# A spectral filter and a gated unit in one kernel: shorter table arithmetic, filter loads without a cast on ScalarE's queue, and an emitted order kept on four engines

## The chip, the cores and the metric

The kernel runs on one core of a Trainium2 chip. The core has five engines that run their own instruction streams in order: PE (TensorE, matrix products), DVE (VectorE), ACT (ScalarE), POOL (GpSimd) and SP (SyncE, which here only issues transfers). Sixteen DMA engines move data for all of them. The metric is the device time of one execution in microseconds, and the number to forecast is the median over several runs.

## The reference, cut to what matters

```python
X = np.fft.rfft(x, axis=1)                    # x: 8 batches, 3200 positions, 256 channels, float32
Y = X * (filt_r + 1j * filt_i)[None]          # 1601 frequencies x 256 channels
y = np.fft.irfft(Y, n=3200, axis=1)           # first layer's output
gate = sigmoid(causal_conv(y, conv_w))        # 5 taps along the positions, per channel
out = ((gate * (y @ w_val)) @ w_out)          # 256 x 256 weights, float32 out
```

## The kernel before

**The transform.** 3200 is 128 x 25, so the transform of a batch is done in two passes of matrix products with tables of cosines and sines that the kernel builds itself. The first pass (`s1`) multiplies the input with the 128-point table `cf_t`; its result goes through a scratch tensor in DRAM, `dscr`, to be read back in another layout. The second pass (`s2`) uses `wc_t`, `ws_t` and `wsn_t`. The product with the filter (`fr_t`, and `fm_t`, which holds the imaginary part with both signs) is three instructions on VectorE: `za` (line 354), `zb` (358), `z` (360). The way back is `inva` with `vc_t`, `vs_t`, `vsn_t`, a second scratch tensor `escr`, and `invb` with `ci_t`. Then come `conv` (20 matmuls into one sigmoid), `val` and `outp`.

**The names.** Each batch is cut into seven chunks, so (b, j) below is chunk j of batch b. A chunk's transfers are called X (input load, line 86, issued by POOL, which casts float32 to bf16 on the way), D (write of `so` to `dscr`, line 312), T (read of `dscr` into `tt`, lines 326 to 329, eight transfers a batch), E (write of `u` to `escr`, line 392, two or three transfers a chunk), V (read of `escr` into `vt`, line 398, seven a batch) and O (output, line 475). SP issues all but X, so these five share one in-order queue.

**The loop.** One pass G of the loop emits, for chunks that are some passes apart, `load_x`, `invb`, `s2`, `conv`, `s1`, `inva`, `val`, `outp`. `s2` runs 9 passes behind `s1`, `inva` 10 and `invb` 19. All seven chunks of `dscr` are read back after the last `s1` of a batch, so T(b) has three passes to arrive before `s2`(b, 0); V(b) has three passes between the last `inva` and `invb`(b, 0).

**Buffers.** PSUM is a pool of four tiles of 128 x 1024 float32, one for each stage of a chunk in turn, so a stage can start when the tile of four stages before is evicted: `invb` needs the eviction of the `s1` before it (`so`, line 310, VectorE). ScalarE evicts `xs` (349), `u` (381), `y` (415) and the gate (436).

**What sets the order.** A scheduler orders the instructions of every engine by its own estimate of times, and then gives each transfer a completion counter. There are eight counters for the transfers of SP and ACT together, taken in turn, and eight for POOL's. A transfer waits until the previous holder of its counter has landed. SP, ACT and POOL stand still in such a wait.

**The preparation.** Before the loop the tables are made. VectorE reduces each angle by `floormod` (seven instructions, lines 103 to 113), ScalarE takes the sine, and VectorE spreads it (`expand`, line 171, 13 instructions a table) and negates it (177). POOL issues the seven X of batch 0, then the 24 filter loads (lines 216 to 225, with a cast to bf16), eight loads of weights (276, 280), and only then X of batch 1. The seven `so` of batch 0 stand on VectorE behind the tables of the second pass. The filter's signs are applied on VectorE (232, 234), as are the 20 `dg_t` instructions (284).

Of the kernel before, what the change touches and what calls it, by code (L numbers as in the profile page):

```python
# [8 lines left out]
FP32 = mybir.dt.float32  # L9
# [6 lines left out]
PI = math.pi  # L16
# [6 lines left out]
R = 25  # L23
# [12 lines left out]
def kernel(  # L36
# [31 lines left out]
    b_npi = cpool.tile([128, 1], FP32, name="b_npi")  # L68
# [5 lines left out]
    tpool = ctx.enter_context(tc.tile_pool(name="s2i", bufs=8))  # L74

# [13 lines left out]
    for j in range(NCH):  # L89
        load_x(0, j)  # L90


    with tc.tile_pool(name="gen", bufs=1) as g1, \
# [3 lines left out]
        def floormod(src_ap, divisor):  # L97
            shp = list(src_ap.shape)
            divi = g2.tile(shp, I32, name=f"fm_i{shp[1]}")
            bak = g2.tile(shp, FP32, name=f"fm_b{shp[1]}")  # L100
            q = g2.tile(shp, FP32, name=f"fm_q{shp[1]}")
            cm = g2.tile(shp, FP32, name=f"fm_c{shp[1]}")
            nc.vector.tensor_scalar(divi[...], src_ap, 1.0 / float(divisor), None,
                                    op0=ALU.mult)
            nc.vector.tensor_copy(bak[...], divi[...])
            nc.vector.scalar_tensor_tensor(q[...], bak[...], -float(divisor), src_ap,
                                           op0=ALU.mult, op1=ALU.add)
            nc.vector.tensor_scalar(cm[...], q[...], float(divisor) - 0.5, None,
                                    op0=ALU.is_ge)
            nc.vector.scalar_tensor_tensor(q[...], cm[...], -float(divisor), q[...],  # L110
                                           op0=ALU.mult, op1=ALU.add)
            nc.vector.tensor_scalar(cm[...], q[...], -0.5, None, op0=ALU.is_lt)
            nc.vector.scalar_tensor_tensor(q[...], cm[...], float(divisor), q[...],
                                           op0=ALU.mult, op1=ALU.add)
            return q

        def iota(shape, pattern, base, cm, name):
            t = g1.tile(shape, FP32, name=name)
            nc.gpsimd.iota(t[...], pattern=pattern, base=base, channel_multiplier=cm,
                           allow_small_or_imprecise_dtypes=True)  # L120
            return t

        nc.vector.memset(b_npi[:, :], -PI)
        pcol = iota([128, 1], [[0, 1]], 0, 1, "pcol")


        kc = iota([128, NG, 2, GL], [[5, NG], [0, 2], [1, GL]], 1, 0, "kc")
        nc.vector.memset(kc[:, NG - 1, 0, GL - 1:GL], 0.0)
        pr = g1.tile([128, NG, 2, GL], FP32, name="pr")
        nc.vector.tensor_scalar(pr[...], kc[...], pcol[:, 0:1], None, op0=ALU.mult)  # L130
        nc.vector.tensor_scalar(pr[:, :, 0, :], pr[:, :, 0, :], 0.75 * L, None,
                                op0=ALU.add)
        q = floormod(pr[...].rearrange("p g c l -> p (g c l)"), L)
        nc.scalar.activation(cf_t[:, :], q[...], AF.Sin, bias=b_npi[:, 0:1],
                             scale=2.0 * PI / L)
# [10 lines left out]
        rq = floormod(pcol[...], R)  # L146
        lp = g1.tile([128, 1], FP32, name="lp")
        nc.vector.tensor_tensor(lp[...], pcol[...], rq[...], op=ALU.subtract)
        nc.vector.tensor_scalar(lp[...], lp[...], 1.0 / R, None, op0=ALU.mult)
        rp = g1.tile([128, 1], FP32, name="rp")  # L150
        nc.vector.tensor_copy(rp[...], rq[...])
# [16 lines left out]
        def expand(dst, src):  # L168
            nc.gpsimd.memset(dst[:, :, P2:128], 0.0)
            for g in range(NG):  # L170
                nc.vector.tensor_tensor(
                    dst[:, g, 0:P2].rearrange("p (l r) -> p l r", l=GL),
                    src[:, g, :].unsqueeze(1).to_broadcast((128, GL, R)),
                    mk[...], op=ALU.mult)

        def negate(dst, src):
            nc.vector.tensor_scalar(dst[...], src[...], -1.0, None, op0=ALU.mult)

        def sincos(prod, dc, ds, dsn):
            qs = floormod(prod[...].rearrange("p g r -> p (g r)"), N)  # L180
            sn = g2.tile([128, NG, R], FP16, name="sn")
            nc.scalar.activation(sn[...].rearrange("p g r -> p (g r)"), qs[...],
                                 AF.Sin, bias=b_npi[:, 0:1], scale=2.0 * PI / N)
            pc = g2.tile([128, NG, R], FP32, name="pc")
            nc.vector.tensor_scalar(pc[...], prod[...], 0.75 * N, None, op0=ALU.add)
            qc = floormod(pc[...].rearrange("p g r -> p (g r)"), N)
            cs = g2.tile([128, NG, R], FP16, name="cs")
            nc.scalar.activation(cs[...].rearrange("p g r -> p (g r)"), qc[...],
                                 AF.Sin, bias=b_npi[:, 0:1], scale=2.0 * PI / N)
            expand(dc, cs)  # L190
            expand(dsn, sn)
            negate(ds, dsn)
# [12 lines left out]
        sincos(kv, wc_t, ws_t, wsn_t)  # L205


        fi_t = gf.tile([128, NG, D], BF16, name="fi_t")

        def fsrc(f, row, ap):  # L210
            return bass.AP(tensor=f.tensor, offset=f.offset + row * D, ap=ap + [[1, D]])
# [340 lines left out]
```

## Time and profile before

| what | value |
|---|---|
| median of 3 runs | 385.33 us (384.27, 385.33, 386.5) |
| profiled execution, its own time | 387.95 us |
| its span in the profile | 385.9 us |
| busy: PE, DVE, ACT, POOL | 312.3, 284.9, 229.1, 64.2 us |
| DMA | 94.53 MB, mean 245 GB/s |
| first `xs` on ScalarE (chunk 0, 0) | starts at 47.12 us |
| first `invb` on PE | starts at 92.66 us |

The profile is one execution. Its busy share of an engine is an average over stages that differ: before 47 us hardly anything but preparation runs, from 93 us to about 300 us all eight stages run side by side, and after that the input side has run out. In the lines of the trace a start time and a duration in microseconds stand first, then the engine, the source line, the operation and its tiles; what stands in brackets is the idle time of that engine before the instruction and what ended it. "SPq" is SP's queue: the duration there is the time that issuing took.

### The profile page before, as it was taken

Reading aid. Unit: us, or ns where it says so; the run is one execution under the profiler, and the core shown is the slowest. Engines: PE = TensorE matmul, PEld = TensorE weight load, DVE = VectorE, ACT = ScalarE, POOL = GpSimd, SP = SyncE. Lnnn points to the kernel's source line nnn. Section 1 sums busy time; section 2 is a strip of 40 time slices with the busy share of each in tenths; the row PEclk is TensorE's granted clock in tenths of the full one; section 3 lists DMA queues with packets and bytes.
Section 4 is the critical chain, followed back from the end, with each engine's and each line's share of the span. In section 5 each row is a group of like instructions: output and inputs, shape, how many; then the busy total and the mean of one; then the engine's idle time right before and its main releaser. Section 6 shows DMA issues by size and latency. Waiting matters only on the chain.

```text
span 385.9 us, 8019 instructions
## 1 busy us (share of the span) xinstructions
PE 312.3 (81%) x3089; PEld 206.9 (54%) x3089; DVE 284.9 (74%) x462; ACT 229.1 (59%) x255; POOL 64.2 (17%) x131
## 2 busy tenths in 40 slices
PE   0230477475899999999997999899999999999992
PEld 0100145253656756766675666566676677666661
DVE  4999958553858887888787789678977677765554
ACT  1100235334976777677765776677677878867660
POOL 8797211112110211021102011100010001001000
PEclk9999998766989999999999999999999999999998
DMA  7999999999999999999999999989595968449343
GB/s 124 144 162 190 216 257 251 231 250 280 179 250 249 311 286 273 263 282 332 274 301 303 286 269 298 285 299 319 201 351 170 304 223 299 136 142 323 141 191 152
DMA packets 94118, 94.53 MB, mean 245 GB/s; under 512 B 10102, under 2 KB 74624, under 8 KB 94080
## 3 DMA queue, kind: packets, MB, share of 16 engines
q1 hardware_dynamic: 80064, 78.98, 62.5%
q0 software_dynamic: 14016, 15.04, 28.1%
q8 instruction: 24, 0.39, 0.4%
q14 instruction: 14, 0.11, 0.1%
HBM read 56.59 MB, written 52.43 MB: 282 GB/s over the span
## 4 chain that ended last, share of the span: by engine, by line
PE 44%; DVE 20%; DMA 19%; SPq 8%; issue 4%; ACT 2%; POOL 1%; DVEq 0%; ACTq 0%; POOLq 0%
PE ps L431 12%; PE ps L448 7%; DMA escr<-u 6%; PE ps L465 6%; DVE so L310 6%; DMA vt<-escr 5%; SPq L326 5%; PE ps L413 5%; DMA dscr<-so 4%; PE ps L376 3%; DVE gv L453 3%; DMA tt<-dscr 3%; PE ps L378 3%; PE ps L307 3%; DVE za L354 2%
## 5 line engine op out<-in xcount | busy, mean ns | idle before, releaser
L415 ACT ACTIVATE yt<-ps 128x1024 bf16<-128x1024 f32 (+1 forms) x56 | 52.1, 931 | 44.3 <-PE ps L413 44.2
L453 DVE TENSOR_TENSOR gv<-ps,gt 128x1024 bf16<-128x1024 f32 (+1 forms) x56 | 61.9, 1104 | 18.7 <-PE ps L448 13.7
L310 DVE CAST so<-ps 128x1024 bf16<-128x1024 f32 (+1 forms) x56 | 61.5, 1103 | 19.0 <-PE ps L307 15.9
L354 DVE TENSOR_TENSOR za<-xs,fr_t 125x1024 bf16<-125x1024 bf16 (+1 forms) x56 | 37.3, 665 | 50.5 <-ACT xs L349 50.3
L381 ACT ACTIVATE u<-ps 125x1024 bf16<-125x1024 f32 (+1 forms) x56 | 53.9, 963 | 24.4 <-PE ps L378 21.6
L431 PE MATMUL ps<-yt,dg_t 64*64 64x512 bf16 (+1 forms) x1120 | 65.7, 361 | 0.8
L349 ACT ACTIVATE xs<-ps 125x1024 bf16<-125x1024 f32 (+1 forms) x56 | 54.0, 965 | 19.6 <-PE ps L346 18.4
L436 ACT ACTIVATE gt<-ps 128x1024 bf16<-128x1024 f32 (+1 forms) x56 | 52.4, 935 | 9.1 <-PE ps L431 5.9
L86 POOL DMA_DIRECT2D xt<-in_x_dram x56 | 30.2, 569 | 153.0 <-PE ps L307 146.5
L307 PE MATMUL ps<-xt,cf_t 128*128 128x512 bf16 x112 | 36.9, 421 | 22.4 <-DVE so L310 11.4
L465 PE MATMUL ps<-wo_t,gv 128*128 128x256 bf16 x400 | 52.8, 273 | 0.9 <-DVE gv L453 0.9
L448 PE MATMUL ps<-yt,wv_t 128*128 128x512 bf16 (+1 forms) x224 | 52.6, 357 | 0.0
L465 PEld LDWEIGHTS <-gv 128*128 128x128 bf16 x400 | 39.1, 98 | 14.9 <-DVE gv L453 1.2
L413 PE MATMUL ps<-ci_t,vt 128*128 128x128 f16 x400 | 31.9, 221 | 13.3 <-DMA vt<-escr 9.6
L431 PEld LDWEIGHTS <-dg_t 64*64 64x64 bf16 x1120 | 30.1, 106 | 23.2 <-issue 10.1
L340 PE MATMUL ps<-tt,wc_t 125*128 125x256 bf16 x104 | 30.1, 289 | 12.9 <-DMA tt<-dscr 10.6
L470 DVE COPY o<-ps 128x1024 f32<-128x1024 f32 (+1 forms) x32 | 36.7, 1148 | 1.1 <-PE ps L465 1.1
L360 DVE TENSOR_TENSOR z<-za,zb 125x1024 bf16<-125x1024 bf16 (+1 forms) x56 | 36.4, 650 | 1.3
L413 PEld LDWEIGHTS <-vt 128*128 128x128 bf16 x400 | 27.0, 98 | 17.9 <-DMA vt<-escr 10.7
L358 DVE TENSOR_TENSOR zb<-xs,fm_t 125x1024 bf16<-125x1024 bf16 (+1 forms) x56 | 36.2, 646 | 0.0
L376 PE MATMUL ps<-z,vc_t 125*128 125x256 bf16 x104 | 30.0, 289 | 6.9 <-DVE z L360 6.9
L307 PEld LDWEIGHTS <-cf_t 128*128 128x128 f16 x112 | 9.2, 108 | 41.7 <-issue 28.2
(109 smaller groups left out, 386.6 us busy)
## 6 DMA issues: line engine op xcount, KB each, us to landing
out_dram<-o SPq DMA_DIRECT2D x32, 512.0 KB
tt<-dscr SPq DMA_DIRECT2D x48, 256.0 KB
escr<-u SPq DMA_DIRECT2D x48, 224.0 KB
out_dram<-o SPq DMA_DIRECT2D x24, 384.0 KB
xt<-in_x_dram POOLq DMA_DIRECT2D x32, 256.0 KB, 6.5
dscr<-so SPq DMA_DIRECT2D x32, 256.0 KB
vt<-escr SPq DMA_DIRECT2D x32, 256.0 KB
xt<-in_x_dram POOLq DMA_DIRECT2D x24, 192.0 KB, 5.7
```

The source lines that it names most:

```text
L307: nc.tensor.matmul(ps[:, a * D:e * D], lhsT=cf_t[:, 0:128], rhs=xt[:, a:e, :], start=True, stop=True)
L310: nc.vector.tensor_copy(so[:, 0:np_, :].rearrange("p a d -> p (a d)"), ps[:, 0:np_ * D])
L349: nc.scalar.activation(xs[0:P2, 0:ng, :, :].rearrange("p g c d -> p (g c d)"), ps[0:P2, 0:ng * 512], AF.Copy)
L354: nc.vector.tensor_tensor(za[0:P2, 0:ng], xs[0:P2, 0:ng], fr_t[0:P2, g0:g0 + ng, :].unsqueeze(2).to_broadcast((P2, ng, 2, D)), op=ALU.mult)
L381: nc.scalar.activation(u[0:P2, 0:2 * ng, :].rearrange("p q d -> p (q d)"), ps[0:P2, 0:ng * 512], AF.Copy)
L413: nc.tensor.matmul(ps[:, o:o + L], lhsT=v[:, a, 128 * dh:128 * dh + 128], rhs=ci_t[:, :], start=True, stop=True)
L415: nc.scalar.activation(y[:, :, H + p0:H + p0 + np_, :].rearrange("p h a n -> p h (a n)"), ps[:, :].rearrange("p (h n) -> p h n", h=2)[:, : ...
L431: nc.tensor.matmul(ps[64 * dh:64 * dh + 64, 512 * r:512 * r + np_ * L], lhsT=dg_t[rows, dh, k, :], rhs=y[rows, dh, p0 + k:p0 + k + np_, :] ...
L436: nc.scalar.activation(g[:, :, 0:np_ * L], ps[:, :].rearrange("p (h n) -> p h n", h=2)[:, :, 0:np_ * L], AF.Sigmoid)
L448: nc.tensor.matmul(ps[:, 512 * eh:512 * eh + np_ * L], lhsT=wv_t[:, dh, 128 * eh:128 * eh + 128], rhs=y[:, dh, H + p0:H + p0 + np_, :], st ...
L453: nc.vector.tensor_tensor(gv[:, :, 0:np_ * L], ps[:, :].rearrange("p (h n) -> p h n", h=2)[:, :, 0:np_ * L], g[:, :, 0:np_ * L], op=ALU.mult)
L465: nc.tensor.matmul(ps[:, D * a:D * a + D], lhsT=gv[:, eh, L * a:L * a + L], rhs=wo_t[:, eh, :], start=(eh == 0), stop=(eh == 1))
```

## The change

**Batch 0 first.** `s1` and `load_t` are defined earlier, so that `s1` of batch 0 is emitted right after `cf_t`, and its `so` alternates between VectorE (even chunks) and ScalarE (odd chunks). T(0) is emitted after the tables of `s2`. POOL makes the two index tiles for `cf_t` after the first X, not after the seventh.

**Tables.** `floormod` is replaced by `sine`: angles are in turns, adding and subtracting 1.5 x 2^23 rounds, and three instructions do what seven did. `expand` is one instruction a table. The negation goes to ScalarE, as do the 20 `dg_t`.

**Filter.** The 24 loads are issued by ScalarE instead of POOL, without a cast, into a float32 tile `ff`; VectorE then makes `fr_t` by one copy and ScalarE makes `fm_t` by two activations with a scale.

**Order.** The loop stands under `manual_schedule` for PE, ACT, DVE and SP, which keeps the order in which it is emitted on these engines. POOL is still ordered by the scheduler.

What stands in the changed program, engine by engine, beside the one before:

- PE and ACT: inside the loop, the same order of stages. PE also has the same number of matmuls.
- VectorE: in the loop before, `so` stands between `zb` and `z` in the passes of chunks 3, 4 and 5 and behind `z` in the four others (from the third batch on); in the changed loop it stands behind `z` in all.
- SP before, where a batch's T are read: D(b, 6), E, O, then the eight T. Changed: D(b, 6), the eight T, then E, O. Where V is read, before: E, O, then V. Changed: E, V, then O.
- ScalarE before the loop, changed: sine for `cf_t`; 5 `dg_t`; `so`(0, 1); first filter load; `so`(0, 3); `so`(0, 5); two sines; second load; negation; 22 loads; two sines; 5 `dg_t`; `fm_t`; negation; `fm_t`; 10 `dg_t`; then the first `xs`.
- Counters: the fourth filter load waits until T(0, 3) has landed, the fifth to the ninth for T(0, 4), the third filter load, T(0, 5) and the two parts of T(0, 6), the tenth and eleventh for D(1, 0) and D(1, 1), and each of the 13 behind them for the load eight places before it.

```diff
+    def s1(b, j):                       # now ahead of the tables; only the eviction differs
...
+        if b == 0 and j % 2 == 1:
+            st[("Sact", j)] = nc.scalar.activation(sov, ps[:, 0:np_ * D], AF.Copy)
+        else:
+            nc.vector.tensor_copy(sov, ps[:, 0:np_ * D])
...
-        def floormod(src_ap, divisor):
...
+        def sine(dst, t):
+            r = g2.tile(list(t.shape), FP32, name=f"sr{t.shape[1]}")
+            nc.vector.tensor_scalar(r[...], t, MAGIC, None, op0=ALU.add)
+            nc.vector.tensor_scalar(r[...], r[...], -MAGIC, None, op0=ALU.add)
+            nc.vector.tensor_tensor(r[...], t, r[...], op=ALU.subtract)
+            nc.scalar.activation(dst, r[...], AF.Sin, scale=2.0 * PI * (1.0 - 2e-7))
...
+        for j in range(NCH):
+            s1(0, j)
...
+        def expand(eng, dst, src):
             nc.gpsimd.memset(dst[:, :, P2:128], 0.0)
-            for g in range(NG):
-                nc.vector.tensor_tensor(
...
+            return eng.tensor_tensor(
+                dst[:, :, 0:P2].rearrange("p g (l r) -> p g l r", l=GL),
+                src[...].unsqueeze(2).to_broadcast((128, NG, GL, R)),
+                mk[...].unsqueeze(1).to_broadcast((128, NG, GL, R)), op=ALU.mult)
 
         def negate(dst, src):
-            nc.vector.tensor_scalar(dst[...], src[...], -1.0, None, op0=ALU.mult)
+            nc.scalar.activation(dst[...].rearrange("p g m -> p (g m)"),
+                                 src[...].rearrange("p g m -> p (g m)"),
+                                 AF.Copy, scale=-1.0)
...
+        for j in range(NCH):
+            load_t(0, j)
...
-        for f, dst in ((filt_r, fr_t), (filt_i, fi_t)):
+        ff = gf.tile([128, 2, NG, D], FP32, name="ff")
+        def load_f(f, c):
+            dst = ff[:, c]
             for l in range(GL):
...
-                nc.gpsimd.dma_start(
+                nc.scalar.dma_start(
                     out=dst[R * l:R * l + HK, 0:ng, :],
...
+        with tc.issue_after(st[("Sact", 1)].ins):
+            load_f(filt_r, 0)
+        with tc.issue_after(st[("Sact", 3)].ins):
+            load_f(filt_i, 1)
...
-        nc.vector.tensor_scalar(fm_t[0:P2, :, 0, :], fi_t[0:P2, :, :], sgn[0:P2, 0:1],
-                                None, op0=ALU.mult)
...
+        with tc.issue_after(vs_ins.ins):
+            nc.vector.tensor_copy(fr_t[0:P2, :, :], ff[0:P2, 0])
+        nc.scalar.activation(fm_t[0:P2, :, 0, :], ff[0:P2, 1], AF.Copy,
+                             scale=sgn[0:P2, 0:1])
+        nc.scalar.activation(fm_t[0:P2, :, 1, :], ff[0:P2, 1], AF.Copy,
+                             scale=sg[0:P2, 0:1])
...
-                    nc.vector.tensor_scalar(dg_t[rows, dh, k, :],
-                                            ident[rows, 64 * r:64 * r + 64],
-                                            cw[rows, dh, k:k + 1], None, op0=ALU.mult)
+                    nc.scalar.activation(dg_t[rows, dh, k, :],
+                                         ident[rows, 64 * r:64 * r + 64], AF.Copy,
+                                         scale=cw[rows, dh, k:k + 1])
...
-    for G in range(total):
+    E = mybir.EngineType
+    with tc.manual_schedule(engines={E.PE, E.Activation, E.DVE, E.SP}):
+        for G in range(total):
...
             c = at(G, 0)
-        if c is not None:
+            if c is not None and c[0] > 0:
                 s1(*c)
```

## The prediction

> **What bounds the kernel now.** I read the page first, then stretches of the timeline, the DMA queues in one stretch, and SP's own queue.
>
> The page's busy shares (PE 81%, DVE 74%) hide three stages. Up to 47.12 us ScalarE evicts nothing of the loop. From there to the first `invb` at 92.66 us PE is busy for 27.91 of 46 us. From 93 us a batch takes about 39.7 us (VectorE's `so` of a batch's last chunk starts at 137.59, 176.43, 216.97 and 256.82), and PE is busy for 37 to 38 of each 40 us.
>
> The start hangs on T(0). The chain that ended last, about 34 us:
>
> ```profile
> 31.03 3.13 DMA dscr<-so
> 34.18 0.37 SPq L326
> 34.60 1.70 SPq L326
> 36.34 0.64 SPq L326
> 37.03 4.30 SPq L326
> 41.37 5.33 SPq L326
> 46.75 4.58 SPq L326
> ```
>
> The last D(0) lands, then issuing six T takes 17 us, because the queue accepts no more. PE has T(0, 0) at 45.09 and then waits for T(0, 1) until 50.53 and for T(0, 2) until 55.27. The DMA queues from 36 to 48 us say who goes first:
>
> ```profile
> q0 software_dynamic: 1204, 2.01, 92.8%
> q1 hardware_dynamic: 942, 0.47, 18.8%
> ```
>
> q0 is POOL's (X of batches 1 and 2), q1 is SP's. The packet counts are nearly equal, but X moved 2.01 MB and T 0.47 MB: as long as X is queued, T gets 0.04 MB per us. From 54 to 56 us, nearly alone, q1 moved 0.60 MB, 0.30 per us.
>
> In the middle, SP's queue and PE around the fourth batch:
>
> ```profile
> 179.19 0.40 SPq L312 DMA_DIRECT2D dscr<-so  x1
> 179.68 1.74 SPq L392 DMA_DIRECT2D escr<-u  x2
> 181.51 0.41 SPq L475 DMA_DIRECT2D out_dram<-o  x1
> 184.18 4.88 SPq L326 DMA_DIRECT2D tt<-dscr  x6
> ...
> 197.63 1.10 SPq L392 DMA_DIRECT2D escr<-u  x2
> 198.83 0.36 SPq L475 DMA_DIRECT2D out_dram<-o  x1
> 203.33 3.72 SPq L398 DMA_DIRECT2D vt<-escr  x7
> ```
>
> ```profile
> 207.27 0.62 PE L413 MATMUL ps<-ci_t,vt 128*128 128x128 f16 x8 [2.43 <-DMA vt<-escr]
> ```
>
> E and O fill the time in which D(b, 6) lands, and T follows at 184.18. From 190.3 to 199.2 SP issues almost without a pause; the last E goes out at 198.73 though its `u` was ready at 193.12; V follows at 203.33, and PE stands 2.43 us for it. The two neighbouring batches have 0.72 and 1.75 us of this, the others next to nothing.
>
> **The change part by part.**
>
> *First T.* POOL's 24 filter issues and their waits (7.69 to 25.63 us) go, so X(1, 0), at 31.79 before, is issued at about 14. X(0) needs POOL and DMA until about 13.5 us (q0 moves 0.41 MB per 2 us, X(0) is 1.6 MB), `so`(0, 6) ends at 15.5 to 16.3, D lands 3.1 us (the chain above) to 4.5 us later, and T(0, 0) is issued at about 20 instead of 34.18. That is 14 us earlier, but X(1) is as close ahead of it as before.
>
> *Last T.* PE's first passes release X(2) too: 14 X tiles, at one per 1.3 us (X issues waiting for landed ones stand 1.2 to 1.5 us apart at 39 to 43 us), occupy q0 from 17 to about 35 us. T(0, 0) took 10.9 us from issue to use, T(0, 1) 16.3: they land at 31 and 36. What is then left of T's 1.67 MB, about 1.1 MB, needs 3.7 us at 0.30 MB per us. The last T lands at about 40, D(1, 0) and D(1, 1), queued behind it on SP, at 42.
>
> *Filter loads.* They leave POOL (15 us of issue) for ScalarE's queue, where everything behind them waits. By the counters the fourth load waits for T(0, 3) (about 38 us), the ninth for the last T, the eleventh for D(1, 1): 42. Thirteen are left. Issuing one has no row on ScalarE; SP's rows bound it by 0.33 us (a D) and 0.9 us (a T in a full queue). I take 0.45 us, nearer the D, since a load has 144 to 169 rows and a D has 128: the last is out at 48 us (46 to 54).
>
> *ScalarE behind them.* Two sines at 0.57, five `dg_t` at 0.25 (from VectorE's row, 255 ns), two `fm_t` of 3328 elements at 3.0 (0.84 ns per element, from `xs`: 1.02 us for 1024, 0.59 for 512), the negation of 1664 elements at 1.6, ten `dg_t`: 1.1 + 1.3 + 6.0 + 1.6 + 2.5 = 12.5. The loads' landing and `vs_t` on VectorE lie beside this. First `xs`: 48 + 12.5 = 60.5 us, against 47.12. What VectorE saves (sines, spreading, signs, 20 `dg_t`: about 19 us) is spent waiting; it covers nothing that is late.
>
> *Ramp.* Once `xs` runs, T(0), X(1) and X(2) are there, and VectorE sets the pace: `za`, `zb`, `z` at 0.61 to 0.69 and `so` at 1.22 make 3.1 us a pass. `so`(1, 6) ends 15 us after the first `xs`, D takes 4 us and T 5 (3.9 and 5.3 at 66 to 76 us before), so `s2`(1, 0) starts 24 to 25 us after the first `xs` (before: 29.3). From there to the first `invb` I keep the 16.2 us of before (76.46 to 92.66): the same D, E and V stand on SP, but for one E of 1 us that now follows T. First `invb`: 60.5 + 24.5 + 16.2 = 101, so **+8.5 us**; with the ends of the issue price 99 to 107.
>
> *T ahead of E.* In the loop SP now stands from D(b, 6) to T with nothing to issue, and the E and O that went out there, 1.74 + 0.41 = 2.15 us, come behind T, into the stretch without a pause. The last E and V of the batch before move by up to that. Below, it can be nothing or a small gain, since D and T travel with less beside them; I take 1.5 us, nearer the full price because that stretch has no slack. Only the three batches in which PE already waits for V pay: **+4.5** (0 to 11 if all five do). O behind V costs nothing: four output buffers are 22 us of passes, the delay some 5.
>
> *`z` ahead of `so`.* In the passes of chunks 3 to 5 `so` starts 0.6 to 0.7 later (one `z`). `invb` of the next pass needs its PSUM tile. In chunks 3 and 4 PE is busy without a gap or waits for V; after chunk 5 the loop `invb`, `y`, `xs`, `za`, `zb`, `z`, `so` is what the pass takes (5.85 us, 176.43 to 182.27), and the delay stays. 0.6 times five batches: **+3** (0 to 9 if all three chunks pay).
>
> *At nothing.* PE and ScalarE keep their loop order. The float32 filter moves 3.28 MB in place of 1.64 into SBUF, at 38 to 49 us, when X has run out and DMA has room; without that cover, 1.64 MB at 0.30 MB per us is 5.5 us.
>
> [...]
>
> **Sum.** 8.5 + 4.5 + 3 = +16 us on the profiled execution's own 387.95 us (span 385.9 and 2.05 around it): 404. The median, 385.33, is 2.6 lower, so the forecast is about **402 us**.
>
> **Rivals.**
>
> *ScalarE is free early.* If T(0) is not held back by X (half of q0's tiles arriving later would do), the loads go out one after another from 15 us: 24 at 0.45 end at 26, the landing and 12.5 us of ScalarE give a first `xs` at 41 to 43. With 41 us of ramp the first `invb` is at 83, 9 us earlier; with the loop's +2 to +7.5 the median is 378 to 384. It decides once the last filter load is out before 39 us, 9 before my 48. For it: T is issued 14 us earlier and VectorE is nearly empty. Against it: the packet counts, and X(1) moved forward just as far as T. 0.17.
>
> *Only the start.* SP's stretch after T absorbs E and O, `so` costs nothing: +5 to +9, 390 to 394. For it: four of the seven later batches show no wait for V. 0.2.
>
> *Dearer issue.* 0.9 us a load on ScalarE and T behind E at the full price: +6 on the start, +3 on the loop, 411. For it: SP's T rows. 0.12.
>
> *Nothing moves.* PE's order is the same, and the middle, 93 to 300 us, could reabsorb a late start if DMA (share 0.97 to 1.03 there) set the pace and ran ahead. Against it: X can run only ten tiles ahead. Within 0.5%: 0.04.
>
> **How the numbers follow.** The forecast's case, both the start and the loop slower (394 to 410), has 0.47; with the two other slower rivals 0.79 slower, 0.04 same, 0.17 faster. 0.5% (1.9 us) is about what a measurement of this kernel can tell from no change. The range leaves out one in ten on each side: 381, inside the first rival, and 412, at the end of the dearer issue. The likeliest case alone has 394 to 410.
>
> **What would show it.** In the changed profile: T(0) issued near 20 us (right: 18 to 23); q0 with as many packets as q1 until 35 us; ScalarE's queue issuing its last filter load at 46 to 50 us, waiting for `tt` and `dscr` transfers; first `xs` at 58 to 63; first `invb` at 98 to 105; PE waiting for V 3 to 4 us in three batches; passes of chunk 5 longer by 0.6 us. The forecast is wrong if the first `xs` comes before 50 us, or if T ahead of E makes T land so much earlier that V gains too.

## The result and the profile after

The changed kernel takes 426.09 us in the median (423.64 to 430.16), the one before 385.91 us in the runs beside it (384.27 to 386.5): a ratio of 1.103, with a 95% interval of 1.096 to 1.110. It is slower, as forecast, but by 40 us and not by 16, and outside the range of 381 to 412. The profiled execution took 423.64 us, its span is 421.9. An execution more than 1.5% longer than the fastest of its kernel does not enter the ratios, and where the profiled one is such, the table of runs below has a dash.

Four times of the profile carry most of what follows: the first `xs` on ScalarE, the first `invb` on PE, the first `invb` of the last batch, and the end.

| | before | after | difference |
|---|---|---|---|
| first `xs` | 47.1 | 75.1 | +28.0 |
| first `invb` | 92.7 | 116.7 | +24.0 |
| first `invb` of the last batch | 349.4 | 385.7 | +36.3 |
| span | 385.9 | 421.9 | +36.0 |

So 24 us are lost in the start, 12 in the loop, and nothing after it; the medians differ by 4 us more than the two profiles, since the profiled execution of before is 2 us above its median and that of after 2.4 us below. (Line numbers of after: D 122, T 136 to 139, `fm_t` 301 and 303, filter loads 256 to 265, `xs` 360, E 403, V 409, `invb` 424, O 486.)

The chain of work that ended last, up to the first `xs` (start, duration, what):

```profile
19.15 6.46 DMA dscr<-so
25.65 0.37 SPq L136
...
27.36 5.04 SPq L136
32.44 3.77 SPq L136
36.25 0.76 SPq L136
37.05 7.24 DMA tt<-dscr
44.31 9.03 DMA ff<-in_filt_r_dram
53.35 6.17 DMA ff<-in_filt_i_dram
59.55 5.39 DMA ff<-in_filt_i_dram
```

Up to 44 us it is the chain that the prediction describes: D, six T, T's landing. Then 20.6 us follow in which the chain is nothing but filter loads: one lands, its counter is free, and the load eight places behind it is issued (the eighth, issued at 44.31, has landed at 53.34 and the sixteenth goes out at 53.35; that one has landed at 59.52 and the twenty-fourth goes out at 59.55). ScalarE's own view of the end of it (the bracket is what ScalarE waited for):

```profile
59.55 0.32 ACTq L265 DMA_DIRECT2D ff<-in_filt_i_dram  x1
59.91 0.48 ACT L155 ACTIVATE cs<-sr 128x325 f16<-128x325 f32 x1 [37.21 <-DMA ff<-in_filt_i_dram]
...
65.08 3.07 ACT L301 ACTIVATE fm_t<-ff,sgn 125x3328 bf16<-125x3328 f32 x1 [3.02 <-DMA ff<-in_filt_i_dram]
...
75.10 1.02 ACT L360 ACTIVATE xs<-ps 125x1024 bf16<-125x1024 f32 x1
```

For 37 us ScalarE computes nothing, though each of its issues takes only 0.30 to 0.66 us: it stands behind loads that have to wait. The DMA queues from 51 to 54 us (packets, MB, share of 16 engines; q10 is ScalarE's) say why:

```profile
q10 hardware_dynamic: 498, 0.45, 86.2%
```

The filter loads are alone on the DMA engines, these are busy, and they move 0.15 MB per us (0.14 to 0.16 in the four stretches of 3 us from 51 to 63 us). From 30 to 36 us it is still X that holds T back, packet for packet:

```profile
q0 software_dynamic: 590, 1.00, 89.1%
q1 hardware_dynamic: 601, 0.30, 23.6%
```

In the loop, SP's queue ahead of the third batch's V, and PE at its end, first in the kernel before:

```profile
138.84 0.34 SPq L312 DMA_DIRECT2D dscr<-so  x1
139.27 1.96 SPq L392 DMA_DIRECT2D escr<-u  x2
141.32 0.41 SPq L475 DMA_DIRECT2D out_dram<-o  x1
144.16 5.05 SPq L326 DMA_DIRECT2D tt<-dscr  x6
...
163.22 4.50 SPq L398 DMA_DIRECT2D vt<-escr  x7
```

```profile
166.73 0.62 PE L413 MATMUL ps<-ci_t,vt 128*128 128x128 f16 x8 [0.72 <-DMA vt<-escr]
```

and after:

```profile
164.51 0.42 SPq L122 DMA_DIRECT2D dscr<-so  x1
170.69 3.51 SPq L136 DMA_DIRECT2D tt<-dscr  x6
...
176.95 0.85 SPq L403 DMA_DIRECT2D escr<-u  x2
...
186.22 2.39 SPq L403 DMA_DIRECT2D escr<-u  x3
193.06 3.19 SPq L409 DMA_DIRECT2D vt<-escr  x7
```

and PE at the end of it:

```profile
195.87 1.04 PE L424 MATMUL ps<-ci_t,vt 128*128 128x128 f16 x8 [5.24 <-DMA vt<-escr]
```

SP issues the last D at 164.5 and stands until 170.7 for its landing. Before, E and O went out in that gap; now they follow T, V comes out at 193.06, 28.6 us behind that D and not 24.4, and PE stands 5.24 us for it, against 0.72 at the same place before. Of the 12.3 us that the loop grew in this profile, waits of PE for V make up 5.5. PE's busy time in the third and fourth batch, 37.1 us each before, is 39.2 and 39.3, at a granted clock of 0.50 for 6.8 us in each; the rest is in shorter waits.

### The profile page after: what moved, and what is told of

It is laid out like the page before. It is cut to its first block, busy times and chain, and to the rows that moved or that the text cites. A ratio compares the mean times of both kernels' runs of the same rounds, so it can differ in the third digit from the quotient of the medians.

```text
span 421.9 us, 7912 instructions
## 1 busy us (share of the span) xinstructions
PE 312.2 (74%) x3052; PEld 206.3 (49%) x3089; DVE 268.5 (64%) x365; ACT 245.7 (58%) x282; POOL 49.0 (12%) x107
## 3 DMA queue, kind: packets, MB, share of 16 engines
q0 software_dynamic: 9472, 13.37, 20.6%
## 4 chain that ended last, share of the span: by engine, by line
PE 37%; DMA 30%; DVE 14%; ACT 7%; issue 6%; SPq 5%; POOL 0%; ACTq 0%; DVEq 0%; POOLq 0%
PE ps L442 9%; DMA escr<-u 9%; PE ps L459 6%; PE ps L476 5%; DMA dscr<-so 5%; DVE so L121 5%; PE ps L424 4%; DMA vt<-escr 4%; DMA tt<-dscr 4%; ACT xs L360 3%; PE ps L387 3%; DVE gv L464 3%; DMA ff<-in_filt_i_dram 3%; DVE za L365 3%; SPq L136 3%
## 5 line engine op out<-in xcount | busy, mean ns | idle before, releaser
L365 DVE TENSOR_TENSOR za<-xs,fr_t 125x1024 bf16<-125x1024 bf16 (+1 forms) x56 | 37.1, 662 | 86.6 <-ACT xs L360 86.6
L121 DVE CAST so<-ps 128x1024 bf16<-128x1024 f32 (+1 forms) x53 | 58.7, 1107 | 5.4 <-PE ps L114 4.3
L387 PE MATMUL ps<-z,vc_t 125*128 125x256 bf16 x104 | 29.5, 284 | 41.4 <-DVE z L371 39.3
L459 PE MATMUL ps<-yt,wv_t 128*128 128x512 bf16 (+1 forms) x208 | 51.7, 355 | 0.9
L424 PE MATMUL ps<-ci_t,vt 128*128 128x128 f16 x400 | 33.1, 226 | 24.8 <-DMA vt<-escr 10.4
L114 PE MATMUL ps<-xt,cf_t 128*128 128x512 bf16 x91 | 32.3, 424 | 18.4 <-DMA xt<-in_x_dram 18.4
L424 PEld LDWEIGHTS <-vt 128*128 128x128 bf16 x400 | 27.9, 101 | 30.4 <-issue 17.0
L387 PEld LDWEIGHTS <-vc_t 125*128 125x128 f16 x104 | 10.4, 100 | 53.0 <-issue 41.4
```

The source lines that it names most:

```text
L121: nc.vector.tensor_copy(sov, ps[:, 0:np_ * D])
L365: nc.vector.tensor_tensor(za[0:P2, 0:ng], xs[0:P2, 0:ng], fr_t[0:P2, g0:g0 + ng, :].unsqueeze(2).to_broadcast((P2, ng, 2, D)), op=ALU.mult)
L387: nc.tensor.matmul(ps[:, oh:oh + D], lhsT=t0[0:P2, g, :], rhs=z[0:P2, a, 0, :], start=True, stop=False)
L424: nc.tensor.matmul(ps[:, o:o + L], lhsT=v[:, a, 128 * dh:128 * dh + 128], rhs=ci_t[:, :], start=True, stop=True)
L459: nc.tensor.matmul(ps[:, 512 * eh:512 * eh + np_ * L], lhsT=wv_t[:, dh, 128 * eh:128 * eh + 128], rhs=y[:, dh, H + p0:H + p0 + np_, :], st ...
```

## The experiments

Stage starts are from the profile of each run, in us; the ratio is to the kernel before on the same chip, with its 95% interval. Differences in the text are to the median of before beside the same run, which was 384.4 to 386.5.

| run | first `xs` | first `invb` | last batch | median | ratio |
|---|---|---|---|---|---|
| before | 47.1 | 92.7 | 349.4 | 385.9 | 1 |
| after | 75.1 | 116.7 | 385.7 | 426.1 | 1.103 (1.096 to 1.110) |
| loop alone | 49.2 | 92.6 | 360.9 | 397.1 | 1.029 (1.023 to 1.036) |
| start alone | 78.8 | 120.7 | 377.5 | 414.2 | 1.071 (1.063 to 1.080) |
| `z` ahead of `so` alone | 49.8 | 90.8 | 352.2 | 390.7 | 1.016 (1.012 to 1.020) |
| T ahead of E alone | 49.3 | 92.0 | 361.6 | 399.0 | 1.031 (1.025 to 1.037) |
| both moves undone | - | - | - | 388.7 | 1.004 (1.000 to 1.009) |
| PE kept busy | 48.2 | 93.8 | 364.5 | 401.2 | 1.036 (1.029 to 1.043) |
| loads on POOL, cast | 45.5 | 91.2 | 360.0 | 397.7 | 1.029 (1.022 to 1.035) |
| loads on POOL, float32 | 54.3 | 100.8 | 370.3 | 407.7 | 1.053 (1.047 to 1.058) |
| loads first on ScalarE | 63.4 | 105.4 | 374.2 | 411.7 | 1.066 (1.059 to 1.073) |
| loads of 16 partitions | 75.8 | 117.8 | 384.4 | 423.1 | 1.102 (1.095 to 1.110) |
| loads of 128 partitions | 63.5 | 105.4 | 374.7 | 412.2 | 1.074 (1.065 to 1.082) |
| X(1) held behind T(0) | 81.6 | 124.7 | 391.8 | 431.2 | 1.121 (1.113 to 1.128) |
| X(1, 2..) held | 81.9 | 123.3 | 391.7 | 431.4 | 1.116 (1.112 to 1.121) |
| imaginary filter first | - | - | - | 384.9 | 0.999 (0.995 to 1.004) |
| and X(1) earlier | 31.9 | 86.1 | 342.2 | 383.6 | 0.994 (0.991 to 0.997) |

**Which part costs what: loop alone, start alone.** The first puts the written order on the kernel before; the second takes it from the kernel after.

```diff
-    for G in range(total):
+    with tc.manual_schedule(engines={E.PE, E.Activation, E.DVE, E.SP}):
+        for G in range(total):
```

> The kernel before, with only the loop run in the order it is emitted (T ahead of E, `z` ahead of `so`); preamble, filter loads and tables are those of before. Theory of the two traces (the start costs 24 us, the emitted loop order 12 us on its own): first `invb` as before, 92 to 93 us, then 10 to 14 us more up to the end, median 396 to 400. The prediction's price for the loop, +7.5: 392 to 395. Rival, the loop's loss was only a consequence of the late start (the prediction's rival `only the start`): within 2 us of before, 384 to 388.

> The changed kernel, with the loop left to the scheduler as before; the filter loads stay on ScalarE's queue in float32 and the tables stay short. Theory (the start alone costs 24 us): first `xs` at 73 to 77 us, first `invb` at 114 to 119, median 408 to 413. Rival, the scheduler's loop takes part of a late start back (SP runs ahead): 400 to 406. Rival, the order written by hand is what made the start late: first `xs` below 65 us and a median below 400.

Measured: +12 and +29 us, together the whole. The loop alone falls into the theory's range and not into that of the prediction's price; the start alone comes out 1 to 2 us above each of the three ranges of its theory. The table shows it in another way. From the first `invb` to the last batch's it takes 256.7 us before, 256.8 with the start alone and 256.1 in the last row, but 266.6 to 269.6 in the nine that have the changed loop whole and in T ahead of E alone (PE kept busy, which adds work, has 270.7; `z` ahead of `so` alone has 261.4). The loop's 12 us do not depend on when the loop starts, and a start that is 28 us late is not made good. The rival "only the start" falls, and so do those that the scheduler's loop would win some of it back and that the order written by hand made the start late: without it the first `xs` is at 78.8 us.

**The loop's two moves.** One run has T behind E, and V behind O, so that only `z` ahead of `so` is left; one puts `z` behind `so` where it was and leaves T ahead of E; one undoes both.

```diff
             if c is not None:
                 s1(*c)
-                if c[1] == NCH - 1:
-                    for j in range(NCH):
-                        load_t(c[0], j)
...
+            c = at(G, 0)
+            if c is not None and c[1] == NCH - 1:
+                for j in range(NCH):
+                    load_t(c[0], j)
```

> As the run with the loop alone in the emitted order, but with T moved behind E, and V behind O, of the same pass, so that SP has the order of before and only `z` ahead of `so` is left. By the prediction's parts (T ahead of E 4.5, `z` ahead of `so` 3): 388 to 390. If SP's order is all of the loop's loss: 384 to 388. If `z` ahead of `so` is all of it: as slow as the run with the loop alone, 396 to 400.

> The kernel before with the loop in the emitted order as in the first run, but with `z` behind `so` in the passes in which the scheduler had it there: VectorE has the order of before, and only T ahead of E and O (and V ahead of O) is left. By the run without T ahead of E (390.7, so 6.5 below the run with both): 390 to 393. By the prediction's price (4.5): 389 to 391. If the two parts only bite together: 385 to 388.

> The kernel before under an order written by hand that undoes both moves: T behind E, V behind O, and `z` behind `so` in the same passes as the scheduler had it. Theory (the two moves are all of the loop's loss): within 2 us of before, 384 to 388. Rival (the hand-written order costs something by itself, or the moves are not the ones named): 390 or more.

Measured: +5.5, +12.5 and +2.7 us. The last is a ratio of 1.004 with an interval that reaches 1.000, and its median of 388.7 lies between the theory's range and the rival's: the two moves are all or nearly all of the loop's loss, and up to 0.9% may be something else in the order written by hand. They do not add, and none of the three ranges for T alone held: T ahead of E costs the whole 12 by itself, and `z` ahead of `so` costs something only where T is not already late. In the profile of `z` ahead of `so` alone, 4.0 of the 4.6 us that the loop grew lie between the second and the third batch, where PE waits 4.22 us for V. What SP waited for, before (total us, times, longest), in the kernel before:

```profile
SPq L326 <- DMA dscr<-so: 15.1, 8, 3.8
SPq L398 <- DMA escr<-u: 13.5, 8, 3.7
```

and in the run with T ahead of E alone (V is line 402 there):

```profile
SPq L326 <- DMA dscr<-so: 31.0, 12, 5.2
SPq L402 <- DMA escr<-u: 21.4, 12, 3.6
```

SP's wait for D's landing doubles, because nothing is issued in it, and what was issued in it comes later. PE's longer waits for V are 6.53, 3.69 and 5.01 us in the third to fifth batch, against 0.72, 2.43 and 1.75: +10.3 of the 12.5 us. How such a wait falls out differs from run to run: with both moves, in the loop alone, the three are 3.43, 3.37 and 1.83.

**PE kept busy.** In the loop alone, PE's clock falls with the two longest waits for V, which end at 170.94 us (PE had stood 3.43 us) and at 214.08 (3.37). The windows of that run (us, PE busy, then the other engines; the third number from the end is the granted clock):

```profile
172.00:174.00 2.00, 2.00 (x24) 0.87 (x22) 0.25 (x1) 1.70 (x2) 1.16 (x2) 0.53 0.86 255
216.00:218.00 2.00, 2.00 (x20) 1.00 (x22) 0.03 (x1) 1.26 (x2) 1.16 (x2) 0.50 0.88 293
```

It looked as if a stall were paid twice. The test fills the stall with matmuls:

```diff
         ps = psum()
+        if j == 0 and b in (2, 3):
+            for _ in range(12):
+                nc.tensor.matmul(ps[:, 0:512], lhsT=wc_t[0:P2, 0, :],
+                                 rhs=fm_t[0:P2, 0, :, :].rearrange("p c d -> p (c d)"),
+                                 start=True, stop=True)
```

> The run with the loop alone in the emitted order (397.1), with 12 matmuls of 512 columns that compute nothing of use ahead of the first `invb` of the batches 2 and 3, where PE there stands 3.43 and 3.37 us for V and is granted a clock of 0.50 to 0.61 in the 4 and 6 us that follow. The added work is 2.6 us in each place, inside the stall. Theory (a stall of over 3 us brings the clock down, and that costs 1.7 and 3 us more): the clock stays at 1.00 there, median 392 to 394. Rival, the clock falls for another reason or costs nothing: 396 to 399, and up to 402 if the added work is not hidden.

The clock stays up, in the same places of this run:

```profile
174.00:176.00 2.00, 2.00 (x34) 1.34 (x31) 0.00 (x0) 1.58 (x2) 0.50 (x1) 1.00 0.89 259
218.00:220.00 2.00, 2.00 (x33) 1.28 (x31) 0.00 (x0) 1.69 (x2) 0.60 (x2) 1.00 0.95 261
```

and the kernel is not faster: 1.036 against 1.029, with intervals that overlap. In these two places the clock was at 0.53 and 0.50 after the stall and at 1.00 where the stall was filled; that this costs 1.7 and 3 us is not borne out. From the third batch's first `invb` to the fifth's, where the clock stayed up, this run takes 85.7 us, and the loop alone, with the clock down twice, 85.9; PE, at a clock of 1.00, waits longer at the next place (2.98 us in the fifth batch, against 1.83). Outside that stretch the clock of this run did fall, from 131 and from 261 us, after waits of 2.69 and 2.98 us (a matmul of 256 columns takes 0.42 us there and 0.27 before and after), so its median does not compare a clock that is up throughout. It looks as if the loop is paced here by the chain through SP and the scratch tensors and not by PE; what the added matmuls cost by themselves was not measured.

**Whose queue, and how many bytes.** The loads go back to POOL, with the cast and without it; the loop is the changed one.

```diff
-                nc.scalar.dma_start(
+                nc.gpsimd.dma_start(
                     out=dst[R * l:R * l + HK, 0:ng, :],
```

> The changed kernel, with the 24 filter loads back on POOL's queue, cast to bf16 on the way as before; short tables, ScalarE's part of the spreading and the emitted loop order stay. Theory (the float32 loads on ScalarE's queue, their issue behind T and their landing, are the start's whole loss): T(0) is again issued at 30 to 35 us as before, but ScalarE is free early: first `xs` at 40 to 48 us, first `invb` at 85 to 93, and with the loop's 12 us a median of 390 to 399. Rival, the shorter tables or the spreading on ScalarE hold the first `xs` back as well: first `xs` above 55 us, median above 404.

> The changed kernel with its float32 filter loads on POOL's queue, ahead of X(1), in place of ScalarE's; so they share no completion counter with D and T, and nothing of ScalarE stands behind their issue. It differs from the run with cast loads on POOL (first `xs` 45.5 us, median 397.7) by the float32 bytes alone. Theory (narrow loads at 0.15 MB per us: 3.3 MB take 22 us, half as many bytes 11): first `xs` 8 to 12 us later than with the cast, 53 to 58, median 406 to 410; against the changed kernel 17 to 22 us earlier, which is then the price of the place on ScalarE's queue. Rival, the bytes cost nothing and the queue is all: first `xs` 44 to 48, median 396 to 400.

Both as the theory had them, but that with the cast T(0) went out at 22.9 us and not at 30 to 35. With the cast on POOL the first `xs` is at 45.5 us and only the loop's 12 us are left. Float32 in place of bf16 costs 8.7 us of first `xs` (9 to 10 us in the median), and the place on ScalarE's queue, behind T and X, another 20.8 (18 to 19 us). So the shorter tables and ScalarE's share of them cost nothing, and the start's loss is the filter loads'.

**Why a load is slow.** The same bytes and the same number of loads, into 16 partitions and into all 128 (with other rows of the filter, as the expectations say).

```diff
-                    out=dst[R * l:R * l + HK, 0:ng, :],
-                    in_=fsrc(f, l + 1, [[L * D, HK], [GL * D, ng]]))
+                    out=dst[:, g0:g1_, :],
+                    in_=fsrc(f, g0, [[12 * D, 128], [D, g1_ - g0]]))
```

> The changed kernel, with the same 24 filter loads on ScalarE's queue and the same 3.3 MB, but each into 16 partitions with 12 rows between two partitions, in place of 13 or 12 partitions (other rows of the filter land there, so its values are not the filter's; all else is computed). In the changed kernel q10, alone on the DMA, moves 0.15 MB per us with the engines at 86%. If the number of partitions sets the number of engines, and that the rate: 0.15 x 16 / 12.5 = 0.19 MB per us at close to 100%, the last load lands 3 to 5 us earlier, first `xs` at 70 to 72, median 421 to 423. If the narrowness of a load (a few partitions written at a time) is what is slow: 0.15 as before, first `xs` at 74 to 76, median 424 to 428.

> As the run with 16 partitions, but each of the 24 loads goes to all 128 partitions, one row (1 KB) each and two in the last of each half (again other rows than the filter's). If loads into few partitions are what is slow, q10 now moves 0.25 to 0.31 MB per us (T's own rate), the last load lands 8 to 11 us earlier than in the changed kernel, first `xs` at 64 to 68, median 412 to 419. If rows of 1 KB from DRAM cost what they cost wherever they land: 0.15 to 0.19 MB per us, first `xs` at 71 to 76, median 421 to 428.

With 16 partitions, 51 to 54 us:

```profile
q10 hardware_dynamic: 107, 0.49, 105.3%
```

With 128 partitions, 45 to 48 us, X and T beside it:

```profile
q10 hardware_dynamic: 552, 0.50, 48.3%
q0 software_dynamic: 108, 0.18, 41.2%
q1 hardware_dynamic: 239, 0.11, 12.4%
```

Float32 loads on POOL, 31 to 34 us, where they too are alone:

```profile
q0 software_dynamic: 216, 0.44, 105.7%
```

With 16 partitions the engines are full and the packets 4.6 KB and not 0.9 KB, and the rate is nearly the same, 0.16 MB per us; on POOL's queue, in packets of 2 KB, it is 0.15. So at busy shares of 86% to 106%, in packets of 0.9, 2 and 4.6 KB and on two queues the rate stays between 0.15 and 0.16. With 128 partitions a packet of 0.9 KB keeps an engine for 42 ns (48.3% of 16 engines in 3 us, over 552 packets) and not 83 (86.2%, over 498); taken over the other stretches it is 41 to 68 ns from 24 us on, against 71 to 94 in the changed kernel from 44 to 63 us. But narrowness by itself does not make the difference: the changed kernel's first two loads, which travelled one at a time beside X and D, took 53 ns a packet; several of them beside X, in the second of the runs that hold X(1), took 83 or more from 39 to 63 us. In these two runs the slow packets are those of several narrow loads in flight together; in the run with the loads first on ScalarE, where eight are out by 6.2 us, a packet took 56 ns from 12 to 15 us and up to 117 ns in the other stretches from 9 to 39 us. So several in flight can be slow and need not be, and what makes them so no run here shows.

How much of the first `xs`, which comes 11.6 us earlier with 128 partitions, is due to the width this run does not show. Its loads also stand elsewhere in ScalarE's order: 13 are out by 22.1 us, ahead of T(0), where the changed kernel has three out by 22.6, so that fewer were left when T(0) had landed. The last one lands at 53.4 and not at 64.9 us. And the rate that was expected for them, 0.25 to 0.31 MB per us, was not seen: beside X and T they got 0.17 at most.

**Is it T(0), held back by X?** The prediction put the loads' delay on T(0), and T(0)'s on X. POOL reads one element of every T(0) tile before it issues X(1), in the second run before it issues the third tile of X(1).

```diff
+        for j in range(NCH):
+            hold_ins = nc.gpsimd.tensor_copy(hold[0:P2, j:j + 1],
+                                             st[("T", 0, j)][0:P2, 0, 0, 0:1])
...
-                load_x(*c)
+                with tc.issue_after(hold_ins.ins):
+                    load_x(*c)
```

> The changed kernel with one wait more: POOL reads one element of each T(0) tile before it issues X(1), so that X(1) does not travel beside T(0). By the prediction's step `Last T` (X holds T(0) back and the filter loads wait behind T(0)): T(0) lands at 30 to 33 us in place of 44, the last filter load goes out at 46 to 50 in place of 59.6, first `xs` at 61 to 66 in place of 75, median 412 to 417. Rival, the filter loads' own time sets the first `xs` wherever T(0) is, or X(1) now collides with them: first `xs` at 72 to 76, median 424 or more.

> As the run that holds X(1) behind T(0), but the first two tiles of X(1) go ahead of the wait, so that D(1, 0) and D(1, 1) can go out before 30 us. In the run before it the tenth and eleventh filter loads stood until 51.4 and 53.4 us, when those two D had landed. Theory (T(0)'s landing and the counters shared with D and T hold the filter loads): the last load out at 46 to 54 us in place of 59.6, first `xs` at 60 to 68, median 410 to 418. Rival, X(1) beside the filter loads costs what T(0) gains: first `xs` at 72 or more, median 423 or more.

Half of it holds. T(0) has landed at 33.5 us and not at 44.3, so X was what held it. But the first `xs` is later, not earlier. The timeline of the first of the two runs:

```profile
33.51 0.48 POOL L275 COPY hold<-tt 125x1 bf16<-125x1 bf16 x2 [2.74 <-DMA tt<-dscr]
35.20 0.30 ACTq L259 DMA_DIRECT2D ff<-in_filt_r_dram  x1
45.30 2.23 SPq L122 DMA_DIRECT2D dscr<-so  x2
51.44 0.33 ACTq L263 DMA_DIRECT2D ff<-in_filt_r_dram  x1
53.35 0.32 ACTq L265 DMA_DIRECT2D ff<-in_filt_r_dram  x1
```

Ten loads are out by 35.2 us. The eleventh and twelfth (the expectation of the second run calls them the tenth and eleventh) stand for 16 us, until D(1, 0) and D(1, 1) have landed, whose counters they need, and these are late since X(1) is. With two tiles of X(1) let through that stall is gone, and X and the loads now share the engines, from 51 to 54 us:

```profile
q0 software_dynamic: 238, 0.41, 77.9%
q10 hardware_dynamic: 188, 0.18, 32.5%
```

The loads get 0.06 MB per us there, and the last lands at 71.9 us. So the rival held in both runs. Whatever is put first, X(1), X(2), T(0) and the narrow loads have to pass the same engines before the first `xs`, as long as the loads come last.

**The loads first, on the same queue.**

```diff
+        load_f(filt_r, 0)
+        load_f(filt_i, 1)
         MAGIC = 1.5 * 2.0 ** 23
...
-        with tc.issue_after(st[("Sact", 1)].ins):
-            load_f(filt_r, 0)
-        with tc.issue_after(st[("Sact", 3)].ins):
-            load_f(filt_i, 1)
```

> The changed kernel with the same 24 float32 loads on the same ScalarE queue, but as the first thing on it, ahead of `cf_t`'s sine, so that X(1), X(2) and T(0) come behind them. `cf_t` waits until the loads are issued, the 8 counters let the last out at 22 to 28 us, and D(0) and T(0) follow it, T(0) from about 36 us. Theory (what cost 28 us is that the loads stood last in the DMA's work, not whose queue they were on): first `xs` at 48 to 56 us, median 400 to 409, as with the float32 loads on POOL (407.7). Rival (ScalarE's queue is the cause wherever the loads stand on it): first `xs` at 65 or later, median 416 or more.

Between the theory and its rival: first `xs` at 63.4, 411.7 us. ScalarE:

```profile
30.88 0.32 ACTq L166 DMA_DIRECT2D ff<-in_filt_i_dram  x1
31.23 1.28 ACT L181 ACT_TABLE_LOAD   x1 [31.23 <-DMA ff<-in_filt_i_dram]
32.52 0.31 ACT L181 ACTIVATE cf_t<-sr 128x130 f16<-128x130 f32 x1
...
41.99 3.07 ACT L300 ACTIVATE fm_t<-ff,sgn 125x3328 bf16<-125x3328 f32 x1 [8.43 <-DMA ff<-in_filt_i_dram]
44.96 1.71 ACT L119 ACTIVATE so<-ps 128x1024 bf16<-128x1024 f32 x2
```

The loads have landed 23 us earlier than in the changed kernel. But ScalarE was kept until the last was issued, so `cf_t` and with it `s1`(0) start at 33 us; then `so` stands behind an `fm_t` that waits for the filter, and T(0) goes out at 58 us. Standing last is part of the cause, and an in-order ScalarE behind waiting loads is another; the run does not part them further.

**A faster kernel?** Cast loads on POOL, the scheduler's loop, the short tables and batch 0 first; on POOL the imaginary filter, three tiles of X(1), then the real filter. The second run also issues the other four tiles of X(1) ahead of the small weights.

```diff
-        load_f(filt_r, 0)
         load_f(filt_i, 1)
+        for j in range(3):
+            load_x(1, j)
...
         sincos(nc.vector, nv, vc_t, vs_t, vsn_t)
+        load_f(filt_r, 0)
+        for j in range(3, NCH):
+            load_x(1, j)
```

> An attempt at a faster kernel from what the first runs showed: cast filter loads on POOL as before, the loop left to the scheduler, the shorter tables and ScalarE's share of the preamble kept, and on POOL the imaginary filter first, then three tiles of X(1), the two short counts, and only then the real filter. In the run with cast loads on POOL ScalarE waited for the imaginary filter until 35.4 us and PE for X(1, 0) until 41. Theory: the imaginary filter lands at about 25 us, first `xs` at 35 to 40, first `invb` at 80 to 88, median 374 to 382. Rival, VectorE or the scratch transfers take the gain back before the first `invb`: 383 to 388.

> The attempt at a faster kernel (imaginary filter first; 384.9, the same as before) with the last four tiles of X(1) issued right behind the real filter, ahead of eight small weight loads. There the first `xs` came at 33 us, but PE waited for X(1, 3) until 45, and VectorE had no `so` from 30 to 46. Theory: `so`(1, 3) comes 4 to 6 us earlier, first `invb` at 82 to 86 in place of 88.7, median 378 to 383. Rival (the scratch transfers of the middle take back any earlier start, as in that run, where 4 us at the second batch were 1 at the fourth): 383 to 387.

The first is as fast as before, as its rival had it. The second is 0.6% faster (0.991 to 0.997), 383.6 us against 386.0 beside it: the one version that comes out ahead of the kernel before, if by little. Its time lies in its rival's range and just outside its theory's. ScalarE:

```profile
24.01 3.07 ACT L301 ACTIVATE fm_t<-fi_t,sgn 125x3328 bf16<-125x3328 bf16 x1 [0.25 <-DMA xt<-in_x_dram]
...
31.87 1.02 ACT L360 ACTIVATE xs<-ps 125x1024 bf16<-125x1024 f32 x1 [1.11 <-PE ps L357]
```

The first `xs` is 15 us earlier than before, the first `invb` 6.6 (in a profiled execution of 380.38 us, the fastest of twelve). The difference is lost in between: PE there waits for T(1) until 70.33 us, 10.8 us at one go.

## Why the prediction was right or wrong

**Right: the sign, and the shape.** Slower in the start and in the loop, with longer waits for V as a part of the loop's share (5.5 of 12.3 us in the profile after), and T(0) held back by X packet for packet. ScalarE stood behind the loads in the way told, up to the eleventh. The ramp was forecast at 40.7 us from the first `xs` to the first `invb` and took 41.6.

**Wrong, 11.5 us and the largest: the step "Filter loads", with the line "At nothing" under it.** It had eleven loads out at 42 us, when D(1, 1) lands, and the last thirteen, at 0.45 us of issue each, at 48. The eleventh was out at 45.79, 3.8 us later; the last thirteen then took until 59.55, 13.8 us and not 6. Issue was cheaper than priced (0.30 to 0.66 us, mostly 0.3 to 0.4), but at 1.1 us a load it was not issue that set the pace, and it was small against the loads' transfers, 5.4 to 9.0 us each in the chain above. The term that was mis-sized is the loads' own travel. The prediction took 0.30 MB per us for it, T's rate into 128 partitions, and called it hidden; alone on the engines they got 0.15, several loads of 12 or 13 partitions being in flight at once, and a load waited for the one eight places ahead of it to land (53.34 and 53.35 us, 59.52 and 59.55). The six T in 17 us are not an issuing price either: the first of them took 0.37 us, the last three 4.3 to 5.3 us each, while T moved 0.04 MB per us beside X; in the second of the runs that hold X(1) back, six T went out in 3.9 us.

**Wrong, 3 us: "ScalarE behind them".** From the last issue to the first `xs` it took 15.5 us and not 12.5. ScalarE's own work from 65.08 on was as priced, but the last landing does not lie beside it: `fm_t` stood 3.0 us for it.

**Wrong, 5.7 and 4.3 us, inside the 11.5: "First T" and "Last T".** T(0) was issued at 25.65 and not at 20: `so`(0, 6) ended at 19.1, and D took 6.46 us beside X. T landed at 44.3 and not at 40. Mending that alone gains nothing: in the two runs that hold X back T is early and the first `xs` is later, in the first since the loads wait for D(1, 0) and D(1, 1), in the second since X takes the engines from them.

**Wrong in size: "T ahead of E" and "`z` ahead of `so`".** Priced at 4.5 and 3, they measure 12.5 and 5.5 alone and 12.0 together. The price of 1.5 us a batch in three batches was too low: with T ahead of E alone PE's waits there grew by 5.8, 1.3 and 3.3 us. The price of `z`, 0.6 us in five batches, had the passes of chunk 5 as its reason; in its own run most of the loss was one longer wait for V. Both moves delay the same chain, from the last `so` over T to V, which would explain that they do not add; that is argued, not shown.

**The rivals.** "ScalarE is free early" needed the last load out before 39 us. "Only the start" is refuted by the loop alone, "dearer issue" by the issue times, "nothing moves" by the result. None had the loads' own travel in it, and so no bound of the range did. Two small slips change nothing: T(0, 1)'s 16.3 us are counted from the issue of T(0, 0), and 404 less 2.6 is 401.

## What to carry to other kernels

Price a load by what loads of its shape took in the trace, with as many in flight, and not by the best rate in it: here T into 128 partitions moved 0.29 MB per us (alone from 27 to 30 us in the second of the runs that hold X(1)), and several loads into 12 or 13 partitions 0.15 (alone from 51 to 54 us in the changed kernel). Where a transfer is issued from a computing engine's queue, price the waits ahead of it as well as the issue: ScalarE computed nothing for 37 us behind issues of 0.30 to 0.66 us, since each load waited for its counter and so for whoever held it. Here the loads were better placed on a queue that had nothing urgent behind them, and ahead of the bulk transfers: the first `xs` was at 54.3 us with them on POOL ahead of X(1), at 63.4 with them first on ScalarE, and at 75.1 as changed. And when two moves delay the same chain, measure them together, since their prices need not add: here 12.5 and 5.5 us alone were 12.0 together.

## What the runs showed of the hardware that was not expected

- Several loads of 12 or 13 partitions in flight, alone on the engines, moved 0.14 to 0.16 MB per us in the changed kernel (51 to 63 us, packets of 0.9 KB, the engines 72% to 86% busy) and 0.15 on POOL's queue (31 to 34 us, packets of 2 KB, 106%), and loads of 16 partitions 0.16 (51 to 54 us, packets of 4.6 KB, 105%). A packet of 0.9 KB kept an engine for 71 to 94 ns in the changed kernel from 44 to 63 us, for 53 ns where one such load travelled at a time, for 56 to 117 ns where the loads came first on ScalarE (9 to 39 us), and for 41 to 68 ns where they went to 128 partitions.
- After waits of PE of 2.5 to 6.5 us ahead of a batch's first `invb` its granted clock mostly fell to 0.50: for 6.8 us in the changed kernel (194.4 to 201.2 and 238.8 to 245.6 us), for about 3.5 us in the run with PE kept busy (131.1 to 134.6, by its matmuls of 0.42 and not 0.27 us). The length of the wait alone does not tell: the matmuls went to 0.42 us after 2.51 us (and X(1) earlier, at 200) and after 2.69 (PE kept busy, at 130), and the clock stayed at 1.00 after 2.43 (before, at 207) and once after 3.69 (T ahead of E alone, at 215). Keeping it up with idle matmuls gained nothing in the two batches in which it did stay up (85.7 us against 85.9).
